# Pair sums of exponentials on GpSimd and a re-ordered opening in a fused attention and gated-feed-forward kernel

## The chip, the cores and the metric

The kernel runs on one core of one Trainium2 chip. The metric is the device time of one execution in microseconds; the number given for a kernel is the median of its runs. The core's engines run their own instruction streams in program order and meet only through semaphores: TensorE (PE; its weight loads appear as PEld), VectorE (DVE), ScalarE (ACT), GpSimd (POOL) and SyncE (SP, which here only issues transfers).

## The reference

Attention with keys and values pooled 4 x 4 over a 384 x 32 image, followed by a feed-forward layer with a ReLU gate:

```python
# q (4, 12288, 128), kv (4, 384, 32, 128), w_sr (128, 128)
kv_pool = kv.reshape(B, H//4, 4, W//4, 4, C).mean(axis=(2, 4))
k = v = kv_pool.reshape(B, -1, C) @ w_sr          # 768 keys per image
s = (q @ k.transpose(0, 2, 1)) / sqrt(C)
a = exp(s - s.max(-1, keepdims=True)); a /= a.sum(-1, keepdims=True)
x = (a @ v).reshape(49152, 128)
out = (maximum(x @ w_gate, 0) * (x @ w_val)) @ w_out   # d_ff = 1536
```

All inputs and the output are float32. Because gate times value is of second degree in x, the kernel leaves x unnormalised and multiplies the output rows by the squared inverse of the row sum of the exponentials.

## The kernel before

The 49152 rows are 96 tiles of 512 (24 to an image). For a tile there are score products (queries against 768 keys), exponentials on ScalarE, value products, then 12 feature blocks of 128: a value projection (`v`, line 504), its copy to SBUF (`y`, line 141 on ScalarE or 143 on VectorE), a gate projection (`g`, line 515), the gated product on VectorE (`h`, line 523) and the output product (`o`, line 545). At the end of a tile the output is turned on VectorE (`oT`, line 553), scaled on GpSimd (line 558) and stored.

From tile 6 on, the order of work is a fixed list of words, `STEADY`, emitted once per tile. The first six tiles and the first image's keys are done by another list, `OPENING`, whose words are emitted one by one by `open_step`. Each word puts one step on one engine. The order of the words is therefore the order on every engine's queue, and `ENGINES` says for some words on which engine they run (`v` VectorE, `a` ScalarE, `p` GpSimd). A number behind `@` names the PSUM bank a step takes; there are eight banks in the opening, of which two become the wide score buffer when `s4.0` comes.

The words that matter here:

- `a`, `b`, `c`: additions of 128 x 512 f32 that sum pixel lines of a chunk of 128 keys (line 272); `p`: the same at 128 x 256, `r`: at 128 x 128. `T`: TensorE turns a chunk, adding up what is left to add (line 300). `kvT`: copy of the turned chunk; `pj`: its projection with w_sr (line 314); `key`: the scaled copy that the scores read; `vt`, `val`: the same as values.
- `cast`, `qt`, `qT`: queries of one tile to f16, turned on TensorE (tiles 0 to 3) and copied. For tiles 4 and 5 `ql` loads the tile (a small memset on GpSimd, then four transfers on SyncE's queue, line 192), GpSimd casts it, and `qT` is a turning transfer. `qd`: loads on GpSimd's queue for tiles 6 and 7 (line 758).
- `S k.j`, `E k.j`, `V k.j`: scores, exponentials and value product of tile k (0 to 3) with chunk j. `xT`: copy of the finished x.
- `U`: the row sums of tiles 0 to 3. For a chunk it is four matmuls with a 128 x 32 block of ones, one per tile, that stand side by side in the array and write to four strips of one PSUM bank (line 474). `R` turns that bank on VectorE, `R2` takes the inverse and squares it (lines 490 and 491), `lsc` spreads it in sixteen small GpSimd copies (line 496) for the first `oT`.
- `gate2.1`: a tiny copy on GpSimd that reads a late line of chunk 4, so that what stands behind it in GpSimd's queue waits for that line; `W0`, `W1`, `wo`: the weights' loads on that queue (lines 744 to 751).
- `D`, `F`: products of no use that fill TensorE while the first lines arrive (lines 738 and 672).
- `s`, `e`: scores and exponentials of tiles 4 and 5 in the steady state's manner (lines 397 and 402). `tq`, `k`, `qn`: further query loads and turning transfers.

In the list before, GpSimd does `r1`, `p2`, `p3`, the gate, the weights, `ql`, the four `qd`, `cast4` and `cast5`. Row sums come as `U0.1` (eight matmuls) and `U2.3.4.5` (sixteen).

Of the kernel before, what the change touches and what calls it, by code (L numbers as in the profile page):

```python
# [16 lines left out]
def kernel(  # L17
# [48 lines left out]
    ENGINES = dict(word.split(":") for word in """
        a0:v a1:v p0:v r0:v b1:v c1:v p1:v kvT0:v r1:p cast0:a cast1:a key0:v kvT1:v qT0:v
        cast2:a cast3:v qT1:v val0:v key1:v qT2:v qT3:v val1:a a2:v a3:v p2:p b3:v c3:v kvT2:a
        p3:p key2:a kvT3:a val2:v a5:v key3:v p5:v a4:v r5:v b4:v val3:a c4:v kvT5:a p4:v key5:v
        kvT4:a val5:v key4:v val4:v xT0:v xT2:v y0.8:v y0.2:a xT1:v y2.0:a y0.10:a cast4:p y0.7:a  # L70
        y0.6:a cast5:p y0.0:a y2.1:a xT3:a y0.1:a y1.10:a y0.5:a y0.4:a y0.3:a y0.9:a y1.8:a
        y1.1:a y1.0:a y0.11:a y1.11:v y1.3:a y2.3:a y1.7:a y1.4:a y2.2:a y2.7:a y2.4:a y1.5:a
        y1.6:a y1.2:a y2.5:v y1.9:a y2.6:a y2.11:a y2.8:a y2.9:a y2.10:a
    """.split())
    OPENING = """
        D1@2 D0@2 F384@2 a0 a1 p0 r0 T0.r@0 T0.3 b1 T0.2 c1 F256@2 p1 kvT0 r1 cast0 pj0@0 T1.r@1
        cast1 qt0@2 key0 kvT1 vt0@0 qT0 qt1@3 cast2 pj1@1 cast3 S0.0@2 qT1 qt2@4 E0.0 qt3@5 val0
        key1 qT3 S1.0@3 E1.0 vt1@1 val1 V0.0@2 S1.1@0 E1.1 S0.1@5 E0.1 qT2 S2.0@4 S2.1@1 V1.0@3
        a2 S3.1@6 V1.1 E3.1 V0.1 S3.0@5 T2.2@0 V3.1@6 p2 E2.1 a3 T2.p V2.1@1 E2.0 b3 T2.3 c3 E3.0
        U0.1@5 kvT2 pj2@0 V2.0 key2 p3 T3.p@4 kvT3 S2.2@0 E2.2 vt2@7 val2 V3.0 gate2.1 S1.2@4  # L80
        E1.2 pj3@7 a5 S0.2@0 V2.2 W0 key3 W1 ql4 ql5 S3.2@4 E0.2 E3.2 p5 V1.2 a4 S3.3@7 S0.3@0
        E3.3 V0.2 T5.2@4 E0.3 r5 T5.r vt3@7 val3 T5.3 kvT5 wo S1.3@0 S2.3@7 b4 c4 p4 V3.3 pj5@4
        V3.2 E1.3 T4.p@0 E2.3 V1.3 key5 vt5@4 S2.5@7 kvT4 val5 pj4@0 key4 E2.5 S0.5@4 E0.5 V0.3
        V2.3 S0.4@0 vt4@7 E0.4 V2.5 val4 S1.4@4 V0.5 E1.4 S2.4@7 V0.4 xT0 E2.4 S1.5@0 E1.5 S3.5@4
        V1.4 V2.4 E3.5 S3.4@7 qd3 xT2 v0.8@2 v0.2@0 E3.4 qd1 V1.5 y0.8 v0.10@4 y0.2 v2.0@1 qd0
        U2.3.4.5 xT1 y2.0 qd2 y0.10 cast4 v0.7@3 R v0.6@1 y0.7 g0.2@4 qT4 g2.0@0 h0.2 v0.0@2 y0.6
        v2.1@3 cast5 g0.7@5 h2.0 V3.5 y0.0 g0.6@4 v0.1@1 qT5 h0.7 V3.4 y2.1 v1.10@2 g0.10@0 h0.6
        xT3 o0.7@5 g0.1@3 y0.1 o0.2 h0.10 o0.6 y1.10 v0.5@4 h0.1 g0.0@1 g2.1@0 y0.5 v0.4@2 h0.0
        o0.10 y0.4 v0.3@3 g0.4@4 h2.1 o0.0 y0.3 g1.10@2 v0.9@1 h0.4 g0.5@0 y0.9 v1.8@3 h1.10 s4.0
        y1.8 o0.4 v1.1@1 h0.5 e4.0 g0.8@2 tq1 g0.9@3 h0.8 g1.8@4 v1.0@0 y1.1 o0.5 h1.8 qn1.8 s4.1  # L90
        y1.0 v1.11@2 g1.0@1 h0.9 e4.1 g0.3@4 v0.11@0 h1.0 o0.8 v1.3@3 y0.11 s4.2 y1.11 y1.3
        g1.1@1 v2.3@0 h0.3 o0.9 e4.2 g0.11@3 g2.2@2 h1.1 o0.1 y2.3 v1.7@4 o0.3 h0.11 v1.4@1 y1.7
        g1.7@0 s4.3 R2 y1.4 o0.11 h1.7 lsc e4.3 k5 g1.3@4 v2.2@1 h1.3 o1.0@3 v2.7@0 y2.2 o1.1 oT0
        o1.7 y2.7 g1.4@4 v2.4@1 h2.2 o1.3 y2.4 v1.5@0 v1.6@5 h1.4 g1.11@2 y1.5 g2.3@1 o1.8 h1.11
        y1.6 v1.2@0 g2.4@4 h2.3 s5.0 y1.2 v2.5@5 g2.6@2 h2.4 e5.0 v1.9@0 o1.10 y2.5 g2.5@1 y1.9
        g1.5@4 s5.1 h1.5 o1.4 e5.1 g1.2@0 v2.6@5 h2.5 g1.6@4 o1.11 y2.6 o1.5 h1.6 v2.11@1 s5.2
        h1.2 y2.11 o1.6 g2.7@4 e5.2 v2.8@5 h2.6 v2.9@0 g1.9@1 h2.7 o1.2 y2.8 g2.8@2 s5.3 h1.9
        y2.9 v2.10@5 g2.9@4 e5.3 h2.8 g2.11@0 o1.9 g2.10@1 h2.9 y2.10 oT1 h2.10 h2.11
    """.split()
# [366 lines left out]

    def lead_sums(chunks):
        for jc in chunks:
            first = "sums" not in x_banks
            if first:  # L470
                x_banks["sums"] = bank([128, T])
            sums_left[0] -= 1
            for k in range(LEAD):
                nc.tensor.matmul(  # L474
                    x_banks["sums"][32 * k : 32 * (k + 1), :], ones, aTs[k][:, jc, :],
                    start=first, stop=sums_left[0] == 0, skip_group_check=True,
                    tile_position=(0, 32 * k),
                )

# [198 lines left out]
    def open_step(word):  # L678
# [19 lines left out]
        elif head == "pj":  # L698
            project_chunk(at[0])
        elif head == "key":  # L700
            keep_keys(word, at[0])
        elif head == "vt":
            turn_chunk_values(at[0])
        elif head == "val":
            keep_chunk_values(word, at[0])
        elif head == "cast":
            q_cast(at[0])
        elif head == "qt":
            q_turn_pe(at[0])
        elif head == "qT":  # L710
            q_turned(at[0]) if at[0] < GRP else q_turn_tile(at[0])
        elif head == "S":
            scores(*at)
        elif head == "E":
            exponentials(*at)
        elif head == "V" and at[0] < LEAD:
            lead_values(*at)
        elif head == "xT":
            lead_kept(word, at[0])
        elif head == "U":  # L720
            lead_sums(at)
        elif head == "R":
            lead_inverse() if at else lead_sums_turned()
        elif head == "lsc":
            lead_scales()
        elif head == "v":
            value_proj(*at)
        elif head == "y":
            keep_value(*at)
        elif head == "g":  # L730
            gate_proj(*at)
        elif head == "h":
            gated(*at)
        elif head == "F":
            fill_less(*at)
        elif head == "D":
            ps = freed(bank([128, 512]))
            nc.tensor.matmul(
                ps, ident, kv_in[0, 0][at[0]].rearrange("p h dw c -> p (h dw c)")[:, 0:512],
                start=True, stop=True,  # L740
            )
        elif head == "W":
            own = slice(at[0] * D_FF // 2, (at[0] + 1) * D_FF // 2)
            nc.gpsimd.dma_start(wv16[:, own], moe_w_val[:, own])
            nc.gpsimd.dma_start(wg16[:, own], moe_w_gate[:, own])
        elif head == "gate":
            nc.gpsimd.tensor_copy(gate, line(2 * at[0], at[1])[:, 0, 0:1])
        elif head == "ql":
            q_load_tile(at[0])
        elif head == "wo":  # L750
            nc.gpsimd.dma_start(wo16, moe_w_out.rearrange("(fb f) c -> f fb c", f=128))
        elif head == "qd":
            q_tiles(1)
            rows = q[0, GRP * T : 2 * GRP * T, :].rearrange(
                "(i t j s) c -> j t i s c", i=GRP, t=32, s=NS
            )
# [1 line left out]
            nc.gpsimd.dma_start(
                q16s[1][32 * j : 32 * (j + 1), 2 * NS :].rearrange("t (i s) c -> t i s c", i=2),
                rows[j][:, 2:],  # L760
            )
# [146 lines left out]
```

## Time and profile before

| | us |
|---|---|
| median of three runs | 1024.46 (1024.46 to 1024.63) |
| span of the profiled execution, first to last instruction | 1022.5 |
| the median over that span | 1.96 |

| engine | busy us | share of span |
|---|---|---|
| TensorE | 1017.2 | 99% |
| ScalarE | 918.5 | 90% |
| VectorE | 869.4 | 85% |
| GpSimd | 524.0 | 51% |

The profile gives no time of its own for the profiled execution beside its span; the 1.96 us between span and median are what lies around the first and the last instruction. Times in rows are microseconds from the span's start; a row of a timeline has the start, the length of a run of like instructions, engine, line, operation, output and inputs with their shapes, the count, and in square brackets the idle time ahead of it with what ended it. A row of the groups has the count, the busy time, the mean in nanoseconds of one, and the idle time ahead of such instructions. TensorE's matmuls overlap in the rows (a 128 x 512 product shows 379 ns and the next one starts 215 ns later), so a stretch's true cost is read from the chain, not from the sum of the rows.

### The profile page before, as it was taken

To read this page: it belongs to the slowest core of one execution; us is meant where nothing else is said; L and a number is where in the kernel's file an instruction comes from. 1 tells how busy PE (TensorE), PEld (TensorE's weight loads), DVE (VectorE), ACT (ScalarE), POOL (GpSimd) and SP (SyncE) were. 2 spreads that over 40 slices of the span, in tenths; PEclk is the share of its full clock that TensorE was granted. 3 is DMA by queue.
4 is the path that set the end of the run, shared out by engine and by line. 5 is a ranking of instruction groups with operands and counts; after the bars stand their busy time and mean duration, and the time that the engine had idled before them with its cause. 6 is when DMAs were issued, how large, how long until landed. Compare 5 with 4: busy or idle time off the path is not lost.

```text
span 1022.5 us, 17480 instructions
## 1 busy us (share of the span) xinstructions
PE 1017.2 (99%) x5021; PEld 485.2 (47%) x5021; DVE 869.4 (85%) x1450; ACT 918.5 (90%) x1927; POOL 524.0 (51%) x1312
## 2 busy tenths in 40 slices
...
GB/s 317 172 171 184 186 211 145 140 122 132 132 198 156 201 164 184 136 116 143 125 134 201 165 186 187 157 131 137 128 130 114 147 122 129 124 119 124 98 91 44
DMA packets 475743, 153.48 MB, mean 150 GB/s; under 512 B 451584, under 2 KB 465920, under 8 KB 475648
## 3 DMA queue, kind: packets, MB, share of 16 engines
...
q10 hardware_dynamic: 432, 1.11, 0.3%
...
## 4 chain that ended last, share of the span: by engine, by line
PE 99%; DMA 1%; DVE 0%; ACTq 0%; issue 0%
PE bank_ps L504 24%; PE bank_ps L515 24%; PE bank_ps L545 24%; PE wide_ps L397 12%; PE bank_ps L439 12%; PE bank_ps L529 1%; DMA kv_in<-in_kv_dram 1%; PE bank_ps L456 1%; PE bank_ps L378 1%; PE wide_ps L336 0%; PE bank_ps L300 0%; PE bank_ps L314 0%; PE bank_ps L474 0%; DVE kv_s L272 0%; PE bank_ps L209 0%; ACTq L246 0%
## 5 line engine op out<-in xcount | busy, mean ns | idle before, releaser
L523 DVE SCALAR_TENSOR_TENSOR hT<-bank_ps,val 128x512 f16<-128x512 f32 x1152 | 727.3, 679 | 104.4 <-PE bank_ps L515 83.7
L141 ACT CAST val<-bank_ps 128x512 f16<-128x512 f32 x1149 | 628.4, 596 | 44.4 <-PE bank_ps L504 23.9
L504 PE MATMUL bank_ps<-xT,wv 128*128 128x512 f16 x1152 | 421.0, 379 | 0.0
L515 PE MATMUL bank_ps<-xT,wg 128*128 128x512 f16 x1152 | 376.3, 379 | 0.0
L545 PE MATMUL bank_ps<-hT,wo 128*128 128x512 f16 x1116 | 348.7, 379 | 0.0
L402 ACT ACTIVATE a<-wide_ps 128x768 f16<-128x768 f32 x368 | 302.2, 821 | 44.0 <-PE wide_ps L397 44.0
L397 PE MATMUL wide_ps<-kv,qT 128*128 128x512 f16 x736 | 179.8, 326 | 0.0
L439 PE MATMUL bank_ps<-aT,kv 128*128 128x512 f16 x552 | 179.0, 379 | 0.0
L558 POOL TENSOR_TENSOR o_sb<-o_t,scale 128x512 f32<-128x512 f32 x89 | 93.2, 1047 | 158.8 <-issue 141.0
L545 PEld LDWEIGHTS <-wo 128*128 128x128 f16 x1116 | 109.1, 98 | 132.1 <-issue 0.5
L515 PEld LDWEIGHTS <-wg 128*128 128x128 f16 x1152 | 112.6, 98 | 122.5 <-issue 0.2
L504 PEld LDWEIGHTS <-wv 128*128 128x128 f16 x1152 | 112.5, 98 | 105.4 <-issue 0.4
L423 POOL COPY scale<-square 32x8 f32<-32x8 f32 x736 | 141.2, 192 | 28.6
L416 POOL TENSOR_TENSOR square<-inverse 128x8 f32<-128x8 f32 x46 | 9.3, 202 | 248.9 <-DVE inverse L414 248.9
L838 POOL DMA_DIRECT2D out_dram<-o_sb x208 | 130.3, 632 | 9.6 <-POOL o_sb L558 7.4
L397 PEld LDWEIGHTS <-qT 128*128 128x128 f16 x736 | 71.9, 98 | 87.0 <-issue 0.2
L447 DVE CAST xT<-bank_ps 128x512 f16<-128x512 f32 x92 | 63.6, 691 | 31.7 <-PE bank_ps L439 31.6
L439 PEld LDWEIGHTS <-kv 128*128 128x128 f16 x552 | 53.9, 98 | 65.2
L402 ACT ACTIVATION_READ_ACCUMULATOR a<-wide_ps 128x1 f32 x368 | 76.1, 207 | 0.0
L553 DVE STREAM_TRANSPOSE o_t<-bank_ps 128x512 f32<-128x512 f32 x93 | 65.4, 703 | 0.3 <-PE bank_ps L504 0.2
...
L256 POOL TENSOR_TENSOR s<-kv_in 128x512 f32<-128x512 f32 x36 | 45.1, 1281 | 0.7
...
## 6 DMA issues: line engine op xcount, KB each, us to landing
...
```

The source lines that it names most:

```text
L141: nc.scalar.copy(to, what)
L397: nc.tensor.matmul(s_ps[:, j0 * 128 : j1 * 128], qT, kv16[:, b, j0:j1, 0:C], start=True, stop=True)
L402: nc.scalar.activation(a16s[k][:, s, :], s_banks.pop(s)[:, 0:J], AF.Exp, scale=qk_scale, accum_out=a_sums[k // 2][:, k % 2, s : s + 1],)
L423: nc.gpsimd.tensor_copy(to[32 * b : 32 * (b + 1), :, :, j], squares[k // 2][32 * j : 32 * (j + 1)])
L439: nc.tensor.matmul(x_banks[k], kv16[:, k // NST, jc, C : 2 * C], aT[:, jc], start=first, stop=x_left[k] == 0,)
L504: nc.tensor.matmul(proj_banks["v", k, fb], wv16[:, fb * 128 : (fb + 1) * 128], xTs[k], start=True, stop=True,)
L515: nc.tensor.matmul(proj_banks["g", k, fb], wg16[:, fb * 128 : (fb + 1) * 128], xTs[k], start=True, stop=True,)
L523: nc.vector.scalar_tensor_tensor(hTs[k][:, fb, :], freed(proj_banks.pop(("g", k, fb))), 0.0, vals.pop((k, fb)), op0=ALU.max, op1=ALU.mult,)
L545: nc.tensor.matmul(o_banks[k], wo16[:, fb, :], hTs[k][:, fb, :], start=first, stop=o_left[k] == 0)
L553: nc.vector.transpose(o_t, freed(o_banks.pop(k)))
L558: nc.gpsimd.tensor_tensor(to, o_by, scale.to_broadcast([128, NS, 4, 32]), op=ALU.mult)
L838: queue.dma_start(*out_moves.pop())
```

## The change

For tiles 0 to 3, GpSimd adds the exponentials of chunks 2 and 3, and those of 4 and 5, into two new f16 tiles (`m`, eight additions of 128 x 512). The tiles use the buffers that held the first four query tiles. The row sums then take these pair sums as chunks 7 and 8: `U2.3.4.5` with its sixteen matmuls becomes `U7` and `Ul8` with four each, `Ul8` being the last to add to the bank. `U0.1` is as before. `add_pairs` is new too, and no word of the list calls it.

The opening list and its engines are written anew. Among what differs: `a0`, `p0`, `r0`, `a1`, `a3`, `cast2` and `cast3` are on GpSimd (`a2`, `b3`, `c3` stay on VectorE); `cast0` is on VectorE; `kvT1`, `key0`, `qT1` and `val5` are on ScalarE; `p3`, `kvT3` and `val1` are on VectorE; the copies `y1.11` and `y2.5` are on ScalarE. `ql5`, `ql4`, `qd3` and `qd2` come before the gate and the weights. The 50 products of scores, values and projections before the first of the late sums are the same ones in both lists. `STEADY`, `DRAIN` and everything behind the opening are unchanged.

```diff
-        a0:v a1:v p0:v r0:v b1:v c1:v p1:v kvT0:v r1:p cast0:a cast1:a key0:v kvT1:v qT0:v
...
+        a1:p b1:v c1:v p1:v cast0:v a0:p p0:p r0:p r1:p cast2:p cast1:a kvT1:a kvT0:v qT0:v key0:a
+        cast3:p key1:v a3:p qT1:a qT2:v val1:v qT3:v val0:v a2:v b3:v c3:v p2:p p3:v kvT2:a key2:a
...
-        D1@2 D0@2 F384@2 a0 a1 p0 r0 T0.r@0 T0.3 b1 T0.2 c1 F256@2 p1 kvT0 r1 cast0 pj0@0 T1.r@1
...
+        a1 F256@0 b1 c1 ql5 D1@7 p1 cast0 D0@2 a0 p0 F384@1 r0 T0.3@3 T0.r T0.2 r1 T1.r@0 cast2
+        cast1 kvT1 qt0@5 kvT0 pj0@4 qT0 key0 pj1@6 cast3 qt1@7 key1 ql4 qd3 a3 S0.0@4 S0.1@1 qt2@2
+        vt1@3 qt3@6 qT1 S1.1@0 qT2 E0.1 S1.0@5 val1 qT3 S2.1@7 E0.0 V0.1@3 vt0@4 S3.1@1 val0 S2.0@6
+        E1.1 a2 S3.0@2 E1.0 E3.1 E2.1 b3 V0.0 V1.1@4 V1.0 T2.2@0 V3.1@5 E2.0 V2.1@1 c3 p2 E3.0 p3
+        T2.p qd2 T2.3 U0.1@2 kvT2 pj2@7 T3.p@6 key2 V2.0 S2.2@0 vt2@7 gate2.1 kvT3 val2 W0 S1.2@6
...
+        E1.3 E2.3 c4 p4 key5 T4.p@7 V1.3 vt5@6 kvT4 val5 S2.5@0 pj4@7 S0.5@6 V3.2 V2.3 key4 E2.5
+        qd1 S0.4@7 vt4@0 V2.5 qd0 val4 m1.1 E0.5 E0.4 S1.4@6 V0.5 S2.4@0 V0.4 xT0 m2.1 S1.5@7 E1.4
+        m3.1 S3.5@6 cast4 E2.4 V1.4 V2.4 S3.4@0 E1.5 E3.5 cast5 v0.2@3 xT2 V1.5 v0.10@7 E3.4 v0.8@6
+        v2.0@1 U7 g0.2@0 xT1 v0.7@4 y0.2 y0.8 y2.0 v0.0@3 g2.0@1 g0.7@6 y0.10 h0.2 qT4 y0.7 V3.4
...
+        h0.1 v0.3@6 y0.5 y0.4 v0.9@1 g0.4@5 y0.3 h0.6 o0.10 y0.9 v1.8@0 g1.10@3 h0.5 s4.0 o0.5
+        g0.9@1 h0.4 h1.10 h0.9 v1.0@5 y1.8 m2.2 g0.8@0 tq1 o0.1 e4.0 v1.1@3 y1.0 m1.2 s4.1 g1.8@1
+        Ul8 v2.2@5 y1.1 v0.11@3 h0.8 e4.1 h1.8 o0.9 o0.6 y0.11 g1.1@0 R v1.11@1 y2.2 o0.4 h1.1
...
+    a_pairs = {}
+
+    def pair_of(k, n):
+        if n not in a_pairs:
+            a_pairs[n] = work.tile([128, LEAD, T], FP16, tag="kv_s2", bufs=2, name="a_pair")
+        return a_pairs[n][:, k]
+
+    def add_chunks(name, k, n):
+        add(name, pair_of(k, n), aTs[k][:, 2 * n], aTs[k][:, 2 * n + 1])
...
-    def lead_sums(chunks):
+    def lead_sums(chunks, last):
...
-                    x_banks["sums"][32 * k : 32 * (k + 1), :], ones, aTs[k][:, jc, :],
-                    start=first, stop=sums_left[0] == 0, skip_group_check=True,
+                    x_banks["sums"][32 * k : 32 * (k + 1), :], ones,
+                    aTs[k][:, jc, :] if jc < NJC else pair_of(k, jc - NJC),
+                    start=first, stop=last and jc == chunks[-1], skip_group_check=True,
```

More of the change, by code (lines that the diff above doesn't have):

```diff
@@ L66 @@
     ENGINES = dict(word.split(":") for word in """
-        a0:v a1:v p0:v r0:v b1:v c1:v p1:v kvT0:v r1:p cast0:a cast1:a key0:v kvT1:v qT0:v
[L68 to L71, printed above, removed]
@@ L72 @@
-        y1.1:a y1.0:a y0.11:a y1.11:v y1.3:a y2.3:a y1.7:a y1.4:a y2.2:a y2.7:a y2.4:a y1.5:a
-        y1.6:a y1.2:a y2.5:v y1.9:a y2.6:a y2.11:a y2.8:a y2.9:a y2.10:a
+        a1:p b1:v c1:v p1:v cast0:v a0:p p0:p r0:p r1:p cast2:p cast1:a kvT1:a kvT0:v qT0:v key0:a
+        cast3:p key1:v a3:p qT1:a qT2:v val1:v qT3:v val0:v a2:v b3:v c3:v p2:p p3:v kvT2:a key2:a
+        kvT3:v val2:v a5:v key3:v p5:v a4:v r5:v val3:a m0.1:p kvT5:a b4:v c4:v p4:v key5:v kvT4:a
+        val5:a key4:v val4:v m1.1:p xT0:v m2.1:p m3.1:p cast4:p cast5:p xT2:v xT1:v y0.2:a y0.8:v
@@ L74 @@
+        y2.0:a y0.10:a y0.7:a m3.2:p y0.0:a y0.1:a xT3:a y2.1:a y1.10:a m0.2:p y0.6:a y0.5:a y0.4:a
+        y0.3:a y0.9:a y1.8:a m2.2:p y1.0:a m1.2:p y1.1:a y0.11:a y2.2:a y1.11:a y1.7:a y1.3:a
+        y1.4:a y1.6:a y2.5:a y2.7:a y2.3:a y1.9:a y2.4:a y1.2:a y2.11:a y1.5:a y2.9:a y2.8:a y2.6:a
+        y2.10:a
     """.split())
     OPENING = """
-        D1@2 D0@2 F384@2 a0 a1 p0 r0 T0.r@0 T0.3 b1 T0.2 c1 F256@2 p1 kvT0 r1 cast0 pj0@0 T1.r@1
-        cast1 qt0@2 key0 kvT1 vt0@0 qT0 qt1@3 cast2 pj1@1 cast3 S0.0@2 qT1 qt2@4 E0.0 qt3@5 val0
@@ L78 @@
[L78 to L95, printed above, removed]
@@ new lines @@
+        E1.1 a2 S3.0@2 E1.0 E3.1 E2.1 b3 V0.0 V1.1@4 V1.0 T2.2@0 V3.1@5 E2.0 V2.1@1 c3 p2 E3.0 p3
+        T2.p qd2 T2.3 U0.1@2 kvT2 pj2@7 T3.p@6 key2 V2.0 S2.2@0 vt2@7 gate2.1 kvT3 val2 W0 S1.2@6
+        V3.0 pj3@7 E2.2 S0.2@0 E1.2 a5 V2.2 S3.2@6 key3 E0.2 p5 E3.2 a4 S0.3@7 V1.2 E0.3 T5.2@0
+        V0.2 W1 r5 S3.3@6 vt3@7 T5.r T5.3 val3 S1.3@7 E3.3 wo m0.1 V0.3 S2.3@6 kvT5 V3.3 pj5@0 b4
+        E1.3 E2.3 c4 p4 key5 T4.p@7 V1.3 vt5@6 kvT4 val5 S2.5@0 pj4@7 S0.5@6 V3.2 V2.3 key4 E2.5
+        qd1 S0.4@7 vt4@0 V2.5 qd0 val4 m1.1 E0.5 E0.4 S1.4@6 V0.5 S2.4@0 V0.4 xT0 m2.1 S1.5@7 E1.4
@@ new lines @@
+        m3.1 S3.5@6 cast4 E2.4 V1.4 V2.4 S3.4@0 E1.5 E3.5 cast5 v0.2@3 xT2 V1.5 v0.10@7 E3.4 v0.8@6
+        v2.0@1 U7 g0.2@0 xT1 v0.7@4 y0.2 y0.8 y2.0 v0.0@3 g2.0@1 g0.7@6 y0.10 h0.2 qT4 y0.7 V3.4
+        v0.1@7 h2.0 V3.5 m3.2 y0.0 g0.0@4 y0.1 v1.10@0 qT5 v2.1@1 h0.7 g0.10@3 g2.1@7 v0.6@6 h0.0
+        h0.10 xT3 v0.5@5 o0.2@4 y2.1 g0.1@1 g0.6@3 o0.7 h2.1 y1.10 m0.2 y0.6 v0.4@0 o0.0 g0.5@7
+        h0.1 v0.3@6 y0.5 y0.4 v0.9@1 g0.4@5 y0.3 h0.6 o0.10 y0.9 v1.8@0 g1.10@3 h0.5 s4.0 o0.5
+        g0.9@1 h0.4 h1.10 h0.9 v1.0@5 y1.8 m2.2 g0.8@0 tq1 o0.1 e4.0 v1.1@3 y1.0 m1.2 s4.1 g1.8@1
@@ new lines @@
+        Ul8 v2.2@5 y1.1 v0.11@3 h0.8 e4.1 h1.8 o0.9 o0.6 y0.11 g1.1@0 R v1.11@1 y2.2 o0.4 h1.1
+        g0.11@2 v1.7@3 g1.0@5 h0.11 y1.11 v1.3@0 s4.2 g0.3@1 y1.7 qn1.8 R2 y1.3 o0.8 g1.11@2 g1.3@3
+        v1.4@0 h1.0 k5 o0.11 h0.3 h1.3 e4.2 v1.6@5 h1.11 s4.3 o1.0@1 y1.4 y1.6 o0.3 g1.6@3 g2.2@0
+        v2.5@5 o1.8 e4.3 v2.7@2 lsc h1.6 s5.0 v2.3@3 h2.2 y2.5 g1.7@5 y2.7 o1.3 v1.9@0 oT0 o1.6
+        g1.4@2 e5.0 y2.3 h1.7 o1.10 h1.4 g2.3@4 y1.9 o1.7 v2.4@5 y2.4 g2.7@3 s5.1 e5.1 o1.1 h2.3
+        g1.9@2 v1.2@0 v1.5@4 h2.7 y1.2 v2.11@5 g2.5@3 s5.2 y2.11 y1.5 h1.9 o1.9 g1.2@2 v2.9@0
@@ L99 @@
+        g1.5@5 h2.5 v2.8@3 g2.11@4 y2.9 h1.2 e5.2 o1.4 y2.8 h1.5 h2.11 o1.11 v2.6@2 g2.4@0 h2.4
+        g2.10@5 y2.6 s5.3 g2.9@4 e5.3 h2.9 g2.6@3 o1.2 g2.8@0 h2.8 v2.10@2 o1.5 y2.10 oT1 h2.10
+        h2.6
     """.split()
```

15 lines of the change are left out of this document (9 added, 6 removed).

## The prediction

> **What bounds the kernel now.** I read the page's busy table first, then the chain that ended last, and then went into the first 60 us, since the diff touches only the opening list and what it calls.
>
> ```profile
> span 1022.5 us, 17480 instructions
> PE 1017.2 (99%) x5021; PEld 485.2 (47%) x5021; DVE 869.4 (85%) x1450; ACT 918.5 (90%) x1927; POOL 524.0 (51%) x1312
> PE 99%; DMA 1%; DVE 0%; ACTq 0%; issue 0%
> ```
>
> TensorE is busy for 99% of the span, and the chain runs through it for 99%. So after the opening the time is TensorE's work back to back: whatever the opening takes longer or shorter is carried to the end one to one, and nothing later gives it back. The question is then how much later or earlier TensorE has worked off the opening list. The table of stretches shows who else is near its limit there (columns after the time: PE, PEld, DVE, ACT, POOL busy us with counts; then clock, DMA share, GB/s).
>
> ```profile
> 12.00:19.00 7.00, 7.00 (x51) 3.68 (x51) 4.75 (x10) 5.23 (x13) 1.77 (x2) 1.00 1.03 410
> 19.00:29.00 10.00, 10.00 (x60) 5.20 (x61) 6.95 (x17) 9.47 (x21) 5.69 (x12) 1.00 1.17 223
> 36.00:58.00 22.00, 22.00 (x108) 10.36 (x107) 20.94 (x37) 21.25 (x47) 15.59 (x39) 1.00 1.06 187
> 58.00:68.00 10.00, 10.00 (x50) 4.65 (x49) 8.47 (x16) 9.40 (x20) 8.51 (x26) 1.00 1.12 196
> ```
>
> Before 19 us the transfers are the limit (410 GB/s); from 19 to 29 ScalarE's exponentials run at 9.47 of 10 us beside TensorE; from 36 to 58 VectorE (20.94 of 22) and ScalarE (21.25 of 22) have almost nothing to spare. The chain of waits names the start of it, and what the row sums cost:
>
> ```profile
> 1.42 7.04 DMA kv_in<-in_kv_dram
> 8.49 0.70 DVE kv_s L272
> 9.21 0.70 DVE kv_s L272
> 9.94 0.42 DVE kv_c L272
> 10.36 0.21 DVE kvT_chunk L143
> 10.62 0.49 PE bank_ps L314 x2
> 17.31 0.55 PE bank_ps L474 x8
> 17.85 0.42 PE bank_ps L314 x2
> 28.98 0.98 PE bank_ps L474 x16
> 29.96 0.54 PE bank_ps L504 x2
> 30.50 0.43 PE bank_ps L515 x2
> ```
>
> **The sums themselves.** Sixteen sum matmuls (L474, the step U2.3.4.5) become eight, in two places (U7, Ul8). The rows give 0.55 us for 8 and 0.98 us for 16, so four side by side cost (0.98 - 0.55) / 2 = 0.215 us and entering the group costs 0.55 - 2 x 0.215 = 0.12 us. Leaving it costs too: the pair behind it takes 0.54 us, the next pair 0.43, so 0.11. Before: 0.12 + 4 x 0.215 + 0.11 = 1.09 us. After: two groups of four, 0.12 + 0.215 + 0.11 = 0.445 each, 0.89 together. The edit saves **0.20 us** of TensorE, not the 0.43 that eight matmuls alone are worth. Bounds: 0.43 (the second entry and exit free) to a loss of 0.03 (them twice as dear as read).
>
> **The additions on GpSimd.** Eight additions (m) of 128x512 in f16 are new; the trace has none in f16. The nearest rows:
>
> ```profile
> L256 POOL TENSOR_TENSOR s<-kv_in 128x512 f32<-128x512 f32 x36 | 45.1, 1281 | 0.7
> L260 POOL TENSOR_TENSOR c<-s 128x256 f32<-128x256 f32 x18 | 13.0, 724 | 1.4
> L264 POOL TENSOR_TENSOR kv_s<-c 128x128 f32<-128x128 f32 x18 | 8.2, 454 | 1.4
> L143 POOL CAST q<-q_late 128x512 f16<-128x512 f32 x2 | 1.2, 609 | 6.4 <-DMA q_late<-in_q_dram 6.4
> 22.72 2.19 POOL L758 DMA_DIRECT2D q<-in_q_dram  x4
> 14.91 1.04 POOL L272 TENSOR_TENSOR kv_c<-kv_s 128x256 f32<-128x256 f32 x1 [4.01 <-PE bank_ps L378]
> 15.42 1.08 DVE L272 TENSOR_TENSOR kv_s<-kv_s,kv_in 128x512 f32<-128x512 f32 x1
> ```
>
> The lower end is the one-input cast of the same size, 0.61 us; the same addition in f32 is 1.28; the upper end is that addition stretched as the 128x256 one was at 14.91, 1.28 x 1.04 / 0.724 = 1.84. I take 1.28, the same operation and count of elements. They matter only where TensorE waits. U7 needs m0.1, m1.1, m2.1, m3.1. GpSimd has issued the weights by 22.72 in this trace (the four q loads follow), and now does m0.1, two q loads (2.19 / 4 = 0.55 each), three more m: 22.72 + 1.10 + 4 x 1.28 = 28.94 us. TensorE reaches U7 behind the same work as it reached U2.3.4.5, at 28.98 and later by what the front below adds. So at 1.28 it just fits: **0 us**, with 0.4 us lost for each 0.1 us that an addition is dearer than 1.3. At 1.84 the four end at 31.18, about 1.8 us behind TensorE. Between U7 and Ul8 the list has 35 products of 512 columns at 0.215 and two score steps of 768 columns (0.32 at that rate), 8.2 us, so Ul8 is reached at about 37.9; behind m3.1 GpSimd has two casts and four additions, 28.94 + 1.22 + 5.12 = 35.3: hidden by 2.6 us; at 1.84, 31.18 + 1.22 + 7.36 = 39.8 against 31.2 + 0.3 + 8.2 = 39.7, the stall at U7 having moved it too.
>
> **The front on GpSimd.** Chunk 0's a0, p0, r0 and chunk 1's a1 move from VectorE to GpSimd, which already has r1.
>
> ```profile
> 6.32 1.29 DVE L272 TENSOR_TENSOR kv_s<-kv_in 128x512 f32<-128x512 f32 x2 [5.41 <-DMA kv_in<-in_kv_dram]
> 8.33 0.33 PE L300 MATMUL bank_ps<-ident,kv_c 128*128 128x128 f32 x1
> 8.49 1.42 DVE L272 TENSOR_TENSOR kv_s<-kv_s,kv_in 128x512 f32<-128x512 f32 x2 [0.21 <-DMA kv_in<-in_kv_dram]
> 12.48 1.26 ACT L381 ACTIVATE aT<-bank_ps 128x512 f16<-128x512 f32 x2 [0.35 <-PE bank_ps L378]
> 13.78 3.12 ACT L381 ACTIVATE aT<-bank_ps 128x512 f16<-128x512 f32 x6
> 18.31 0.28 ACT L321 ACTIVATE kv<-bank_ps 128x128 f16<-128x128 f32 x1 [0.70 <-PE bank_ps L314]
> 19.07 3.14 ACT L381 ACTIVATE aT<-bank_ps 128x512 f16<-128x512 f32 x6
> ```
>
> In this trace the lines arrive at 6.32, chunk 0's sum reaches TensorE at 8.33, and the chain goes through VectorE for chunk 1 (b1 from 8.49). In the new list GpSimd runs a1, a0, p0, r0 in that order: 6.32 + 1.28 + 1.28 + 0.72 + 0.45 = 10.05 at the least. T0.2 stands behind T0.r, and kvT0 and pj0 behind that: four transposes (0.5), the copy (0.21 on the chain), some 0.1 of handing over: pj0 at about 10.9 against 10.62, 0.3 us late. That is if VectorE's b1, c1, p1 don't disturb it. At 14.91 they do: the two additions overlap and take 1.04 instead of 0.72 and 1.08 instead of 0.70, as if one stood still while the other ran. If all of a0, b1, p0, c1, p1, r0 take turns, the front costs up to another 1.1 us (VectorE's 0.70, 0.70 and 0.42 make 1.82, less the 0.7 or so in which b1 would have waited for its line anyway): pj0 at 12.0.
>
> The Trainium skill, SBUF — State Buffer, Who interferes with whom, says that a VectorE instruction with two SBUF inputs contends with a GpSimd instruction that reads SBUF, and that the pair of ports is an exclusive lock. By that rule pj0 comes at the 12.0 end, and this edit costs the opening up to 1.4 us before slack. The row at 14.91 agrees with it.
>
> I take the turn-taking for most of it, the first exponential at 13.3 instead of 12.48 (0.8 late; qT1 now also stands ahead of it on ScalarE). Not all of this lasts. Eight exponentials of 0.52 us (3.12 / 6) can run before chunk 2's keys; they end at 16.90 in this trace and ScalarE then has waits until 19.07. Now they end at 13.3 + 8 x 0.52 = 17.45; U0.1 needs the last of them, and pj2 follows at 17.45 + 0.05 + 0.55 = 18.05 instead of 17.85: 0.2 late.
>
> ```profile
> 14.07 1.29 DVE L272 TENSOR_TENSOR kv_s<-kv_in 128x512 f32<-128x512 f32 x2 [0.39 <-DMA kv_in<-in_kv_dram]
> 16.65 0.65 PE L300 MATMUL bank_ps<-ident,kv_in 128*128 128x128 f32 x4
> 42.14 0.24 DVE L490 RECIPROCAL inverse<-sums_turned 128x16 f32<-128x16 f32 x1
> ```
>
> The same happens once more for chunks 2 and 3: a3 is on GpSimd too, ahead of p2 and behind cast2, cast3 and one load (over by 13.4, before the lines of 14.07). 14.07 + 1.28 + 0.72 = 16.07 alone, 16.9 if it takes turns with a2 and b3; T2.p then delays T2.3, which had its line at 16.65, by 0 to 0.3. Together **+0.3 us** at 19 us, bounds 0 (the slack holds it all) and +0.9 (the first exponential's 0.8 passes on whole, and 0.1 of this).
>
> **Other engines.** In 19 to 29 us ScalarE takes val5 (0.2) and is rid of kvT3: with 0.53 us idle there, **+0.1**, 0 to 0.3. Later y1.11 and y2.5 go from VectorE to ScalarE: 2 x 0.52 = 1.04 us onto an engine with 0.75 us idle in 36 to 58 us, and 0.60 more per 10 us after that. The excess is worked off by 68 us, but banks can hold TensorE while it lasts: **+0.15**, bounds 0 and +0.6. VectorE loses as much, which helps h. The sums' bank stays taken from U0.1 to Ul8, 8 us longer, and s4.0 now follows h0.5, the ninth gated product (9.08 / 15 = 0.605 us each, row below), from some 30.5 us on, so at 35.9, where TensorE would be at 29.7 + 28 x 0.215 = 35.7: **+0.1**, 0 to 0.5.
>
> ```profile
> 30.75 9.08 DVE L523 SCALAR_TENSOR_TENSOR hT<-bank_ps,val 128x512 f16<-128x512 f32 x15
> 19.22 0.19 POOL L747 COPY gate<-kv_line 128x1 f32<-128x1 f32 x1 [0.96 <-DMA kv_line<-in_kv_dram]
> 21.28 0.66 PE L300 MATMUL bank_ps<-ident,kv_line 128*128 128x128 f32 x4
> ```
>
> **Queues.** ql5 and ql4 (eight loads of 64 KB) go out on SyncE's queue right behind the kv lines instead of from 21.74; behind them on that queue stand only transposes needed after 30 us. qd3 and qd2 pass gate2.1, W0, W1 and wo on GpSimd's queue: two issues of 0.55 us ahead of the weights, covered by the wait for kv_line until 19.22, and some 128 KB at 410 GB/s, 0.3 us, ahead of the last kv lines. Chunk 5 has its lines at 19.2 and is turned at 21.28, so this is covered; without that cover it is 0.3. The weights go no later and wo has two loads fewer behind it. R now stands behind Ul8, at about 38.5 instead of 30, still ahead of the reciprocal's 42.14. Cost **0**.
>
> **Sum:** -0.20 + 0 + 0.3 + 0.1 + 0.15 + 0.1 = +0.45 us on a span of 1022.5, that is 1022.95. The three runs' median, 1024.46, lies 1.96 us above this span (what lies around it); so I expect 1024.9.
>
> **Rivals.**
> *The reorder closes gaps (faster).* From 10.62 to 28.98 TensorE's chain holds pieces longer than their work: 0.49 and 0.42 for pairs that take 0.22 elsewhere. If the new order fills about 1 us of such gaps and the front's delay is absorbed: -0.2 - 1.0 + 0.2, 1023.5. For it: the slack at 17 us is real. Against: the first link became longer.
> *GpSimd's additions are late (slower).* U7 on TensorE waits for m3.1, and g0.2 and all projections stand behind it. At 1.84 us an addition the stall is 31.18 - 28.98 - 0.4 = 1.8 us: 1024.46 + 0.45 + 1.8 = 1026.7. It passes the bound from 1.80 us an addition. Against it: VectorE's two-input additions are over by 23 us, and a steady row of 1.28.
> *The clock drops (slower).* The fillers now stand ahead of T0.3, and between F384's end at about 8.4 and pj0 at 11 to 12 TensorE has only transposes.
>
> ```profile
> L663 PE MATMUL bank_ps<-ident 128*128 128x512 f32 x4 | 3.8, 1102 | 1.4 <-POOL ident masks.py:199 1.4
> L738 PE MATMUL bank_ps<-kv_in,ident 128*128 128x512 f32 x4 | 2.4, 677 | 0.1
> ```
>
> The same shape took 1102 ns at the start and 677 a little later, so a slow start exists. If TensorE ran at 677 / 1102 = 0.61 of its speed after 12 us for as long as those first four took, 3.8 x 0.39 = 1.5 us of work would be lost on top of the sum: 1026.4, and 1027.0 with the front at its dear end. The Trainium skill, TensorE: Matmul & The Clock Gate, Part 1, says that an idle window of about 3.4 us puts the array back to half rate; no run here shows the case. Against this rival: the gap is at most 3.6 us and holds transposes, and the granted clock is 1.00 in every stretch quoted.
> *ScalarE takes over as the limit after 30 us.* All of its bounds together (+0.3 + 0.6 + 0.5) with the front's +0.3 and -0.2: +1.5, 1026.0. For it: 21.25 of 22 us; against: 58 to 68 us has room.
> *The sums were hidden anyway.* Then only the order counts: 1025.1, within the forecast's range.
>
> **Chances.** Forecast (and the last rival) 0.52, own range 1023.9 to 1025.8; gaps closed 0.16; additions late 0.12; clock 0.08; ScalarE 0.12. The bound of 0.2% (2.05 us: 1022.41, 1026.51) is about what a measurement of this kernel tells from no change. Faster takes a quarter of the first rival, 0.04; slower takes the late additions (0.10), most of the clock (0.05), and 0.03 of ScalarE's: 0.18; the rest, 0.78, is within. For 8 in 10 the range leaves out the far part of the gaps closed and of the late additions: 1023.4 to 1026.9.
>
> **What would show it.** U0.1 still x8 near 17.5 us, then two groups of x4, each of about 0.34 and with 0.11 behind it; the GpSimd additions at 1.28; the first exponential near 13.3; TensorE at U7 near 29.4 without a wait for GpSimd; ScalarE's busy time in 36 to 58 us nearer to 22. Wrong makes it: a wait of TensorE for a_pair, an f16 addition far from 1.28, or a granted clock under 1.00 after 12 us.

## The result, and the profile after

| | median us | runs | span of the profiled execution |
|---|---|---|---|
| before | 1024.55 | 1024.46 to 1024.66 (4) | 1022.5 |
| after | 1034.29 | 1032.23 to 1034.75 (4) | 1032.9 |

The ratio is 1.0089, 95% interval 1.0076 to 1.0102: slower by about 9.7 us by the medians. The forecast was 1024.9.

The chain of waits of the changed kernel, at the places that were shown of the old one and at the one that is new (start us, length us, what):

```profile
8.60 1.05 DVE kv_s L274
9.67 1.10 DVE kv_s L274
10.80 0.57 DVE kv_c L274
11.44 0.58 POOL kv_c L274
13.94 0.85 PE bank_ps L380 x2
19.95 0.55 PE bank_ps L486 x8
26.19 5.26 DVE kv_c L274
31.59 0.66 PE bank_ps L302 x2
39.37 0.33 PE bank_ps L486 x4
39.70 0.32 PE bank_ps L528
48.08 0.33 PE bank_ps L486 x4
48.41 0.54 PE bank_ps L517 x2
```

One row stands out: a VectorE addition of 128 x 256 that took 0.43 us before takes 5.26. It is p4, chunk 4's pixel addition. T4.p on TensorE needs it, and TensorE's queue stands behind T4.p. Its row in the old kernel's timeline:

```profile
22.71 0.43 DVE L272 TENSOR_TENSOR kv_c<-kv_s 128x256 f32<-128x256 f32 x1
```

The other marks are late too: U0.1 (L486 x8) at 19.95 instead of 17.31, the late sums at 39.37 instead of 28.98. From there on the two kernels run at nearly one pace: 39.37 - 28.98 = 10.39 us, and the spans differ by 1032.9 - 1022.5 = 10.4.

VectorE's timeline of the changed kernel around that row, and then GpSimd's (start us, length us, what, and in brackets what ended a wait):

```profile
23.91 2.24 DVE L274 TENSOR_TENSOR kv_s<-kv_s,kv_line 128x512 f32<-128x512 f32 x2
26.19 5.25 DVE L274 TENSOR_TENSOR kv_c<-kv_s 128x256 f32<-128x256 f32 x1
```
```profile
24.44 1.16 POOL L274 TENSOR_TENSOR a_pair<-aT 128x512 f16<-128x512 f16 x1 [1.22 <-ACT aT L383]
25.57 1.11 POOL L777 DMA_DIRECT2D q<-in_q_dram  x2
26.69 3.37 POOL L274 TENSOR_TENSOR a_pair<-aT 128x512 f16<-128x512 f16 x3
30.01 1.16 POOL L145 CAST q<-q_late 128x512 f16<-128x512 f32 x2
```

p4 starts at 26.19 and ends at 31.44. In that time GpSimd runs m1.1, m2.1, m3.1 and both casts back to back, until 31.17; p4 ends 0.27 us behind the last of them. b4 and c4 (23.91, two rows in one) meet m0.1 in the same way and take 2.24 us where before they took 1.41.

At the front the two engines meet too, and there it looks different. GpSimd's rows for a0, p0 and r0, to be read beside the first three rows of the chain above (b1, c1 and p1 on VectorE):

```profile
7.83 1.26 POOL L274 TENSOR_TENSOR kv_s<-kv_in 128x512 f32<-128x512 f32 x1
9.17 1.05 POOL L274 TENSOR_TENSOR kv_c<-kv_s 128x256 f32<-128x256 f32 x1
10.30 0.78 POOL L274 TENSOR_TENSOR kv_c<-kv_c 128x128 f32<-128x128 f32 x1
```

In order of their ends these are a0 9.09, b1 9.65, p0 10.22, c1 10.77, r0 11.08 and p1 11.37: the engines take turns, one addition each. Each GpSimd addition there reads what the one before it wrote, and its row starts 0.08 us behind that one's end.

The stretches (columns as in the prediction: PE, PEld, DVE, ACT, POOL busy, clock, DMA share, GB/s):

```profile
12.00:19.00 7.00, 6.93 (x41) 4.51 (x41) 3.87 (x10) 4.99 (x11) 4.07 (x8) 0.76 1.04 399
19.00:29.00 10.00, 7.29 (x49) 4.21 (x48) 8.46 (x12) 5.40 (x13) 8.55 (x14) 1.00 1.22 262
29.00:36.00 7.00, 4.41 (x14) 2.40 (x15) 3.16 (x4) 2.32 (x5) 2.16 (x3) 0.56 0.64 99
36.00:58.00 22.00, 22.00 (x108) 9.75 (x107) 20.06 (x34) 21.44 (x45) 12.14 (x29) 0.98 0.48 102
```

The granted clock is 0.76 in 12 to 19 us and 0.56 in 29 to 36; in the old kernel it was 1.00 in both. In the chain a score product (L380) takes 0.43 us at 13.94 where it took 0.215.

So three things are to be told apart: the wait for p4, the slow clock (twice), and a later front.

### The profile page after: what moved, and what is told of

Read it like the earlier page. It is cut to its first block, busy times and chain, and to the rows that moved or that the text cites. A ratio compares the mean times of both kernels' runs of the same rounds, so it can differ in the third digit from the quotient of the medians.

```text
span 1032.9 us, 17477 instructions
## 1 busy us (share of the span) xinstructions
PE 1020.5 (99%) x5013; PEld 488.2 (47%) x5013; DVE 872.9 (85%) x1442; ACT 918.9 (89%) x1929; POOL 539.2 (52%) x1326
## 4 chain that ended last, share of the span: by engine, by line
PE 98%; DVE 1%; DMA 1%; issue 0%; ACTq 0%; POOL 0%; DVEq 0%
PE bank_ps L517 24%; PE bank_ps L528 24%; PE bank_ps L558 23%; PE wide_ps L399 12%; PE bank_ps L441 12%; PE bank_ps L542 1%; DMA kv_in<-in_kv_dram 1%; DVE kv_c L274 1%; PE bank_ps L380 1%; DVE kv_s L274 0%; PE bank_ps L458 0%; PE wide_ps L338 0%; PE bank_ps L302 0%; PE bank_ps L316 0%; PE bank_ps L211 0%; PE bank_ps L486 0%
## 6 DMA issues: line engine op xcount, KB each, us to landing
kv_line<-in_kv_dram SPq DMA_DIRECT2D x4, 512.0 KB, 10.2
```

## The experiments

Each version was timed together with the old kernel, whose median then lay between 1024.17 and 1024.45; that is the time it is held against.

Theory A: a VectorE addition with both inputs in SBUF stands still while GpSimd has instructions that read SBUF, not for one of them but until GpSimd's queue runs dry; the additions that the change puts there hold p4, TensorE waits, and the wait slows its clock. Rival B: the front on GpSimd is late, and the rest follows from that. Rival C: the eight additions are dear wherever they stand.

### Without the additions

```diff
-        ... wo m0.1 V0.3 ...  m1.1 ... m2.1 ... m3.1 ... U7 ... m3.2 ... m0.2 ... m2.2 ... m1.2 ... Ul8
+        ... wo V0.3 ...                               ... U2.3 ...                              ... Ul4.5
```

> The changed kernel without the eight additions on GpSimd; the row sums read the raw exponentials in the same two places (eight matmuls each), everything else in the new order. Theory A (VectorE's addition p4, 5.25 us long in the changed kernel, stands still while GpSimd runs additions back to back behind it): only the two casts are left to hold it, so p4 takes at most 1.7 us, TensorE's wait for it falls from 5.3 to at most 1.7 us, the granted clock between 29 and 36 us is 1.00 again, and the time is about 1027.5 (1034.3 less some 4 for the wait and 2.4 for the slow clock behind it, and 0.4 more for the sums). Rival B (the later front and its slow clock are the cause, the additions don't matter): still 1033 to 1035. Rival C (the additions are all of it): 1025 or less.

Measured: 1026.72 (1025.22 to 1027.18, ten runs) against 1024.17; ratio 1.0020, interval 1.0011 to 1.0030. Its VectorE timeline, and then its stretches:

```profile
24.99 0.42 DVE L274 TENSOR_TENSOR kv_c<-kv_s 128x256 f32<-128x256 f32 x1
```
```profile
12.00:19.00 7.00, 7.00 (x44) 4.74 (x45) 3.94 (x10) 5.09 (x11) 4.20 (x7) 0.77 1.03 392
29.00:36.00 7.00, 7.00 (x39) 2.92 (x38) 6.33 (x11) 7.00 (x16) 0.68 (x2) 1.00 0.78 155
```

p4 takes 0.42 us, TensorE doesn't wait for it, and the second slow stretch is gone while the first is still there (0.77). Some 7.6 us of the loss hang on the additions (1034.29 - 1026.72); 2.5 us don't (1026.72 - 1024.17). Rival B is out as the main cause, and so is rival C's claim to all of it.

### p4 on GpSimd, all additions kept

```diff
-        kvT3:v val2:v a5:v key3:v p5:v a4:v r5:v val3:a m0.1:p kvT5:a b4:v c4:v p4:v key5:v kvT4:a
+        kvT3:v val2:v a5:v key3:v p5:v a4:v r5:v val3:a m0.1:p kvT5:a b4:v c4:v p4:p key5:v kvT4:a
```

> The changed kernel with one step moved: p4, chunk 4's addition of 128x256, from VectorE to GpSimd, ahead of the additions m1.1 to m3.1 in GpSimd's own order. Theory A: p4 takes 0.7 to 1.1 us there, TensorE waits about 1 us for it in place of 5.3, no second slow stretch of the clock, about 1027.5. Rival B: no change, 1034. A third reading, that p4 is slow because of its own data or engine queue: it is slow on GpSimd too, 1034.

Measured: 1026.42 (1026.22 to 1027.47, seven runs) against 1024.17; ratio 1.0025, interval 1.0014 to 1.0036. GpSimd's timeline:

```profile
24.77 0.72 POOL L274 TENSOR_TENSOR kv_c<-kv_s 128x256 f32<-128x256 f32 x1 [0.74 <-DVE kv_s L274]
26.55 3.38 POOL L274 TENSOR_TENSOR a_pair<-aT 128x512 f16<-128x512 f16 x3
```

One letter in the list takes back 7.9 us (1034.29 - 1026.42). The additions are as many and as long as before. What cost the time was not their work but the addition that they kept waiting.

### GpSimd waits for p4, which stays on VectorE

```diff
+        elif head == "z":
+            nc.gpsimd.tensor_copy(gate, pixels[at[0]][:, 0, 0:1])
...
-        E1.3 E2.3 c4 p4 key5 T4.p@7 ...
+        E1.3 E2.3 c4 p4 z4 key5 T4.p@7 ...
```

> The changed kernel, p4 on VectorE as there, with one tiny copy more on GpSimd that reads p4's result, ahead of qd1, qd0 and m1.1: GpSimd waits for p4, so no addition stands behind it. Theory A: p4 takes 0.42 to 0.7 us, TensorE waits 0.5 to 1.3 us for it, 1026.0 to 1027.5, as with p4 on GpSimd. If p4 on VectorE were slow by itself, or the two loads qd1 and qd0 held it: p4 stays long and so does the time, 1033 or more.

Measured: 1026.83 (1026.07 to 1027.77, ten runs) against 1024.45; ratio 1.0022, interval 1.0013 to 1.0031. p4 is 0.42 us on VectorE (24.68 to 25.10). So it isn't VectorE's own slowness; it is what stands beside it.

### The wait behind the loads, and behind one addition

In the kernel above both the loads qd1 and qd0 and the additions were kept away from p4. In the next two the same small copy stands further back in GpSimd's queue: once behind the two loads and ahead of m1.1, once behind m1.1 and ahead of m2.1. The diff is that of the first; in the second z4 and m1.1 change places.

```diff
-        qd1 S0.4@7 vt4@0 V2.5 qd0 val4 m1.1 E0.5 ...
+        qd1 S0.4@7 vt4@0 V2.5 qd0 val4 z4 m1.1 E0.5 ...
```

> As before, with the copy that waits for p4 behind the two loads qd1 and qd0 and ahead of m1.1: of what stands behind m0.1, only the loads run beside p4. If the additions hold p4 and the loads don't: p4 0.42 to 0.6 us, 1026 to 1027.5. If the loads hold it too (p4 began 0.5 us ahead of m1.1's row and was held all the same): p4 lasts until the loads end, some 0.5 to 1.2 us.

> The changed kernel with a tiny copy on GpSimd that reads p4's result, now between m1.1 and m2.1: GpSimd's queue runs dry behind m1.1 until p4 is through. Theory A (VectorE's addition stands until GpSimd has nothing from SBUF to run): p4 ends about 0.3 us behind m1.1, so it is some 2 to 2.3 us long in place of 4.7 to 5.3, and the time lies between that with no addition ahead (1026.8) and the changed kernel: 1028 to 1031. If p4 is held by a single long block that has nothing to do with the number of additions behind it: 4.7 us or more again, 1032 to 1035.

Measured: behind the loads 1026.57 (1026.10 to 1027.37, eight runs; ratio 1.0022, interval 1.0012 to 1.0033); behind one addition 1029.44 (1029.11 to 1030.57, four runs; ratio 1.0052, interval 1.0037 to 1.0067), against 1024.38. VectorE's timeline and then GpSimd's, of the kernel that waits behind the loads:

```profile
24.67 0.43 DVE L274 TENSOR_TENSOR kv_c<-kv_s 128x256 f32<-128x256 f32 x1
```
```profile
24.01 1.11 POOL L781 DMA_DIRECT2D q<-in_q_dram  x2
25.23 0.19 POOL L770 COPY gate<-kv_c 128x1 f32<-128x1 f32 x1
```

and the same two of the kernel that waits behind one addition:

```profile
26.15 1.95 DVE L274 TENSOR_TENSOR kv_c<-kv_s 128x256 f32<-128x256 f32 x1
```
```profile
26.65 1.16 POOL L274 TENSOR_TENSOR a_pair<-aT 128x512 f16<-128x512 f16 x1
28.24 0.18 POOL L770 COPY gate<-kv_c 128x1 f32<-128x1 f32 x1 [0.43 <-DVE kv_c L274]
```

The loads run beside p4 without touching it (0.43 us, while they are issued from 24.01 to 25.12). One addition holds it until that addition is over: m1.1 ends at 26.65 + 1.16 = 27.81, p4 at 28.10, 0.29 us later. With five instructions in a row it was the end of the fifth, and 0.27 us. So p4 waits for the end of an instruction of GpSimd, and in the changed kernel it got no turn between any two of the five that stood ready.

Theory A's "until GpSimd's queue runs dry" is too strong, though. In the two kernels below that fill TensorE at the front, or before T4.p with six products, p4 gets in one instruction sooner, between the two casts. GpSimd's row of the one with the front filled, whose p4 runs from 24.58 to 29.25:

```profile
28.37 1.35 POOL L145 CAST q<-q_late 128x512 f16<-128x512 f32 x2
```

A cast takes 0.60 us, so the first ends at 28.97; p4 ends 0.28 us behind that, and the two casts together take 1.35 us where back to back they take 1.16. In five profiles with p4 held, VectorE never got in between two additions m or between m3.1 and the first cast, and twice it got in between the casts. At the front it got in each time. That the 0.08 us gap behind each of GpSimd's additions lets it in there is likely and not shown, and why the two casts differ from profile to profile stays open.

Another thing stays open: p4's row starts 0.5 us ahead of m1.1's and it needs 0.42, and still it is held. That the additions begin on a part of GpSimd while the loads are still issued would explain it; no run here shows that.

### The front back on VectorE

```diff
-        a1 F256@0 b1 c1 ql5 D1@7 p1 cast0 D0@2 a0 p0 F384@1 r0 T0.3@3 T0.r T0.2 r1 T1.r@0 cast2
+        D1@7 D0@2 F384@1 a0 a1 p0 r0 T0.r@3 T0.3 b1 T0.2 c1 ql5 F256@0 p1 cast0 r1 T1.r@0 cast2
...
-        a1:p ... a0:p p0:p r0:p
+        a1:v ... a0:v p0:v r0:v
```

> The changed kernel with the front of the old one: a0, a1, p0, r0 on VectorE and first in the list, the rest in the new order, additions included. If the front on GpSimd is what starts it all: pj0 near 11 us instead of 12.6, clock 1.00 throughout, chunk 4's p4 done by 24 us before GpSimd's additions run back to back, and 1024.5 to 1025.5. If the additions collide with p4 whatever the front does: p4 still 4 us or more, and 1031 to 1033.

Measured: 1032.52 (1031.36 to 1032.93, four runs) against 1024.17; ratio 1.0077, interval 1.0061 to 1.0094. The clock in 12 to 19 us is 1.00 again, U0.1 comes at about 18.0, and p4 is held as before, from 24.55 to 29.77:

```profile
24.55 5.22 DVE L274 TENSOR_TENSOR kv_c<-kv_s 128x256 f32<-128x256 f32 x1
```

The collision doesn't need the late front; the front with its slow clock is worth 1.8 us (1034.29 - 1032.52).

### Filling TensorE's wait at the front

```diff
-        ... r0 T0.3@3 T0.r T0.2 ...
+        ... r0 T0.3@3 F384@1 F384@2 T0.r T0.2 ...
```

> The changed kernel with two more products of no use (128x384 f32, 0.81 us each) in TensorE's wait between T0.3 and T0.r, which lasts 1.9 us. If the slow clock of 12 to 19 us (0.76) comes from TensorE having had only transposes and waits since 8.6 us, the clock there is 1.00, the scores at 13.9 us take 0.22 instead of 0.43 us, and U0.1 comes 1 to 1.9 us sooner than 19.95. Then p4 starts sooner too; theory A says its length depends on what GpSimd does at that moment, so the time is anywhere from 1025.5 (p4 through before the additions) to 1032.8 (still behind them). If the clock has another cause: 0.76 as before and 1034.

Measured: 1032.52 (five runs: four from 1032.20 to 1032.94, one of 1026.08) against 1024.17. Its stretch, and then its chain of waits:

```profile
12.00:19.00 7.00, 7.00 (x59) 4.38 (x57) 4.54 (x10) 5.38 (x12) 4.25 (x7) 1.00 1.03 394
```
```profile
13.11 0.55 PE bank_ps L380 x2
18.06 0.55 PE bank_ps L486 x8
24.58 4.68 DVE kv_c L274
29.40 0.66 PE bank_ps L302 x2
37.17 0.33 PE bank_ps L486 x4
```

With two products of no use in the wait, T1.r and pj0 still hang on GpSimd's r1, but the clock is 1.00 and U0.1 comes at 18.06 instead of 19.95. Of these 1.89 us, 0.36 are there at T1.r already (11.71 for 12.07): b1 took 0.71 us in this execution and 1.05 in that of the changed kernel. The remaining 0.75 us to the old 17.31 aren't the clock. The chain runs through the front here, but the front is not their only cause: with the front back on VectorE, U0.1 comes no sooner than 18.0 (the last experiment shows why). This run alone doesn't settle it, since the first stretch is not slow in every execution of a kernel with this front: in the kernel with p4 on GpSimd the seven runs fall into two groups, four of 1026.22 to 1026.42 with a mean clock of 1.000 and three of 1027.35 to 1027.47 with 0.998, and the profiled one (1.000) has U0.1 at 18.11. Those two groups show the price best: 1.2 us between their middles. The odd run of 1026.08 was not profiled; that p4 slipped past the additions there is likely by its time and not shown.

### Filling TensorE's wait for p4

The diff is that of the kernel with four products of no use between key5 and T4.p; the other has six.

```diff
-        E1.3 E2.3 c4 p4 key5 T4.p@7 ...
+        E1.3 E2.3 c4 p4 key5 F512@6 F512@6 F512@6 F512@6 T4.p@7 ...
```

> The changed kernel with six products of no use (128x512 f32) on TensorE in front of T4.p, so that its wait for p4 (5.3 us) is filled with work. p4 and the additions are untouched. If the slow clock from 31.6 to 36.5 us (granted 0.56 in 29 to 36) comes from that wait: p4 still about 5 us, TensorE's T4.p still near 31.6, clock 1.00 behind it, and 2.2 to 2.5 us less than the changed kernel, about 1032. If the wait is all of the loss and the clock costs nothing: 1034. If p4 itself were held by something on TensorE, p4 would change too.

> As the run with six products of no use in front of T4.p, with four: each took 1.18 us from one to the next there, so that six lasted 7.1 us and held T4.p 2.5 us longer than p4 did. Four end with p4 (about 29.5 where p4 begins at 24.7). From T4.p to the first late sums 5.3 us as there, not 7.8; clock 1.00 in 29 to 36; the time 2.0 to 2.5 us less than the changed kernel's, 1030 to 1032.5. If the clock behind the wait cost nothing: 1034.

Measured: six 1033.29 (1032.60 to 1034.50, four runs; ratio 1.0088, interval 1.0074 to 1.0102) against 1024.45; four 1031.58 (1030.10 to 1032.40, four runs; ratio 1.0066, interval 1.0049 to 1.0083) against 1024.38. Six were too many: one takes 1.18 us to the next, they lasted until 31.90 while p4 was over at 29.36, and what the clock gave the fillers took. The chain of waits of the kernel with four, and then its stretches:

```profile
26.21 5.26 DVE kv_c L274
31.52 0.44 PE bank_ps L302 x2
37.05 0.33 PE bank_ps L486 x4
```
```profile
12.00:19.00 7.00, 6.84 (x42) 4.66 (x41) 3.84 (x10) 4.86 (x11) 4.19 (x8) 0.76 1.04 400
29.00:36.00 7.00, 6.74 (x27) 2.88 (x28) 4.08 (x6) 3.87 (x9) 2.18 (x3) 1.00 0.67 103
```

p4 is held for the same 5.26 us and T4.p comes at the same time (31.52 against 31.59). From T4.p to the late sums it takes 5.53 us (5.32 with six), in the changed kernel 39.37 - 31.59 = 7.78. The clock behind the wait is worth 2.3 to 2.5 us; in time, 1034.29 - 1031.58 = 2.7, where the four runs of the kernel with four products mix two with the slow stretch at the front and two without (mean clock 0.998 and 1.000).

The kernel that waits behind one addition shows a shorter wait. TensorE stands 2.0 us in front of T4.p there, the clock behind it is 1.00, and from T4.p to the late sums it takes 5.50 us. Its chain and its stretch:

```profile
28.25 0.41 PE bank_ps L302 x2
33.75 0.33 PE bank_ps L486 x4
```
```profile
29.00:36.00 7.00, 7.00 (x37) 3.16 (x37) 4.62 (x9) 6.92 (x16) 5.17 (x7) 1.00 0.58 83
```

### The old order with four additions

```diff
-        ... T4.p@0 E2.3 V1.3 key5 ...        U2.3.4.5
+        ... T4.p@0 E2.3 V1.3 m1.1 m2.1 m0.1 m3.1 key5 ...        Ul7.4.5
```

> The old kernel in its old order with one part of the change: GpSimd adds the exponentials of chunks 2 and 3 of tiles 0 to 3 (m1.1, m2.1, m0.1, m3.1, behind wo), and the late sums take the pair sums and chunks 4 and 5 in one place (12 matmuls for 16). The additions come behind E1.3, near 23.4 us, when p4 is done (23.14). Theory A: no VectorE addition from SBUF is left to be held, no wait on TensorE, the sums save one group of four, 0.215 us: 1024.0 against 1024.2, or no difference that can be seen. Rival: additions on GpSimd cost VectorE (the gated products, copies from PSUM) wherever they run: 1025 or more.

Measured: 1024.29 (1024.07 to 1024.97, eleven runs) against 1024.45; ratio 0.9998, interval 0.9990 to 1.0007. Twelve sum matmuls take 0.76 us in its chain for the 0.98 of sixteen, four additions take 4.49 us on GpSimd from 23.55, behind p4 (22.78 to 23.20), and nothing waits for them. VectorE's gated products are as long as they were (9.08 us for fifteen). So these four additions are free where they meet no VectorE addition from SBUF, and worth 0.2 us of TensorE, which the times can't tell from nothing.

### The three places together

The front on VectorE as above, p4 on GpSimd, and m0.1 behind p4:

```diff
-        ... wo m0.1 V0.3 ... c4 p4 key5 T4.p@7
+        ... wo V0.3 ... c4 p4 m0.1 key5 T4.p@7
```

> Three moves on the changed kernel together: the front (a0, a1, p0, r0) on VectorE and first as in the old kernel, p4 on GpSimd, and m0.1 behind p4 instead of ahead of c4. All eight additions stay. If the three named places hold the whole loss: c4 0.7 us, no wait on TensorE over 0.5 us between 12 and 36 us, and 1024.0 to 1024.8. If the new order loses elsewhere too (loads ahead of the last key lines, the sums' bank, ScalarE's two copies more): 1025 to 1026.

Measured: 1025.25 (1024.98 to 1025.77, eleven runs) against 1024.45; ratio 1.0008, interval 0.9999 to 1.0017. That is the second reading (1025 to 1026): the named places hold nearly all of the loss and not the whole of it. The median is still 0.8 us above the old kernel's, though the interval just takes in no difference. The chain of waits shows where U0.1 is held:

```profile
14.61 1.34 DVE kv_s L274
16.09 1.05 POOL kv_c L274
17.18 0.88 PE bank_ps L302 x6
18.06 0.55 PE bank_ps L486 x8
```

It goes through a2 (1.34 us beside a3 on GpSimd) and p2 to T2.p, and U0.1 stands at 18.06 for the old 17.31. With the front on GpSimd the chain reaches the same 18.06 through the front, without a wait of TensorE from T1.r on; these are two ways of nearly one length, and taking away one leaves the other. That a3 on GpSimd is what is left here is read from the chain; no run puts it back on VectorE. No version here beats the old kernel by more than the runs can tell.

## Why the prediction was wrong

**What bounds the kernel**: right. TensorE carries the delay of the opening to the end (10.39 us at the late sums, 10.4 in the span).

**The sums**: right. Two groups of four take 0.33 us each, and the pair behind them 0.54 for 0.43 (48.41): 0.44 a group, 0.21 us saved, for the 0.445 and 0.20 worked out.

**The additions on GpSimd**: here it failed. Their price was close (1.14 to 1.17 us for the 1.28 taken) and U7 did not wait for them, as forecast. But the step priced them at TensorE's U7 alone and called the rest nothing. What they cost was on VectorE, in p4, and from there a wait of TensorE of 5.3 us and the slow clock behind it. The rival on late additions even named the condition and dismissed it: "VectorE's two-input additions are over by 23 us". That was read from the old trace, where p4 is done at 23.14. In the new order p4 starts at 26.19 (24.6 at full clock), and the additions were not asked for p4 but for their place in GpSimd's queue, right beside it. The old row at 14.91 and the rule beside it, The Trainium skill, SBUF — State Buffer, Who interferes with whom, were used for the front, and as a stretch of GpSimd's own additions, but not for what those do to VectorE. They had to be asked for every pair of a GpSimd instruction and a VectorE addition that the new list can bring together.

**How long such a wait lasts** was underpriced as well. The prediction stretched an instruction by the old row's ratio, as if two took turns. At the front they do. Beside the additions m they don't: one addition ahead made p4 1.95 us, three additions and two casts 5.25. The Trainium skill, SBUF — State Buffer, SBUF: two separate sides, says that the one that starts first gets the pair of ports for the whole instruction and the other fully blocks; the runs agree as to the whole instruction (p4 ends 0.27 to 0.29 us behind the end of GpSimd's), and add that GpSimd's next ready instruction can go first again. As to who is first the rows don't decide: p4's row starts ahead of m1.1's.

**The front**: the mechanism was right and the size off. The term, with a3 in it, was +0.3 us, bounds 0 to +0.9; at full clock it measured 0.75 to 0.8 at U0.1 (18.06 and 18.11 for 17.31), and 2.64 in the profiled execution. The turns came as described; the first exponential came at 13.70 at full clock instead of 13.3. a3's share, priced at 0 to 0.3, was too small: with the front on VectorE it alone leaves U0.1 at 18.06.

**The clock**: a rival at 0.08 and 1.5 us. It happened twice in the profiled execution, worth 1.2 us in time at the front and 2.3 to 2.5 us behind p4's wait. The front needed no full stop: from 8.6 to 12.4 us TensorE had transposes and waits only. Two products of no use there kept the clock, in the one profile of that kernel. The Trainium skill, TensorE: Matmul & The Clock Gate, says in Part 1 that about 3.4 us without work set the array to half rate; the stretch at 0.56 behind a wait of 5.3 us, its being gone with the wait filled, and the 1.00 behind a wait of 2.0 us agree.

**Other engines and queues**: ScalarE's two copies and the sums' bank show no wait of TensorE of their own in the profiles of after. The loads ahead of the last key lines cost more than said: with the front on VectorE, c4 waits 0.2 us for its line until 22.9. It is small and inside the terms given.

**The sum**: +0.45 forecast. In the profiled execution: front 0.75, the slow clock there with b1's longer wait 1.9 (19.95 - 18.06), p4's wait 5.3, the slow clock behind it 2.46 (7.78 - 5.32), less 0.2 for the sums, 10.2 of the 10.4.
